# A recurrent attention and two MLPs on one core: fewer operations on the SBUF port that VectorE and GpSimd share, and an order of work that counts that port

## The chip, the cores and the metric

The kernel runs on one NeuronCore of one Trainium2 chip. The metric is the device time of one execution in microseconds (us). Five engines have queues of their own and run them strictly in order: TensorE (PE, with its weight loads shown as PEld), ScalarE (ACT), VectorE (DVE), GpSimd (POOL), and SyncE (SP), which here only starts DMAs.

## The reference

An attention with a matrix state per head (batch 4, 8 heads, 768 steps, head size 40) is followed by two MLPs over the 3072 tokens of width 320:

```python
for t in range(S):
    y[:, :, t] = np.einsum('bhd,bhde->bhe', rt, state)
    Sa = np.einsum('bhde,bhe->bhd', state, at)
    state = state * wt[:, :, None, :] - np.einsum('bhd,bhe->bhde', Sa, bt)
    state = state + np.einsum('bhd,bhe->bhde', vt, kt)
h = np.maximum(x @ w_in, 0.0)
x = h * h @ w_out                      # d_ff 2048
silu = g * (1.0 / (1.0 + np.exp(-g)))  # g = x @ w_gate, val = x @ w_val, d_ff 1536
out = silu * val @ w_out
```

The r, k, v, w, a and b of the attention are float32. The MLP weights reach the kernel as float64, in an array of 64-bit words, and are converted on the chip.

## The kernel before, in words

**Attention.** Time is cut into chunks of 32 steps. One *slot* handles one chunk for half of the batch and all heads. There are 48 slots, and slot i needs the state that slot i-2 left. Ahead of each slot, `e_stage` (L701) loads the decays and a, k, b into a tile called wakb and prepares them: a scan over the decays gives the running products DT (L711), two products give AB ("am", L715), a second, reversed scan over the same decays (L717), a reciprocal of the last running product (L720), a product with it ("rd", L721), and two products that give KB ("km", L724). `inverse` (L755 on) inverts triangular blocks with 30 small VectorE operations (L770, L773) for every window of up to four slots. `slot` then runs the chain on TensorE and VectorE: UQ (L885), TV (L897), ut (L914), the new state ("decay", L916), and the output yb (L954).

**MLP 1** works in 96 *pairs* (12 blocks of 256 tokens by 8 pairs of 128 hidden columns). The operand of every product is split in a rounded high part and a low part, and three products replace one. A pair (`pair1`, L1018) is: 16 matmuls F into one of two PSUM banks (L417), relu from PSUM to the SBUF tile room (L1030), square in SBUF (L1031), the high part gh (a rounding copy, L393), the low part gl = value - gh on GpSimd (`split_pair`, L1013, recorded at L1015), and 12 matmuls O (L422). The PSUM bank is free for the next but one pair as soon as the relu has read it.

**MLP 2** works in 72 pairs of the same kind (`pair2`, L1271 on), with a sigmoid and two VectorE products (L1286, L1288, L1289) in place of relu and square. It runs after the attention's SBUF has been given back. Its weights, converted earlier to float32 in DRAM, are loaded in 48 tiles (`w2_tile`, L1209, low part at L1221).

**Weight conversion.** `conv` (L1070) takes one weight tile of float64 words: 36 tiles for MLP 1 and 36 for MLP 2. `conv_ops` (L366) makes float32 out of the words with eight operations: two on ScalarE (L375, L376), a maximum on VectorE or GpSimd (L377), a shift, a merge and a mask on VectorE (L379, L382, L384), a product and a sum on either engine (L386, L387). ScalarE and GpSimd then make high and low parts ("wh", "wl" at L1099 to L1109).

**The order of the work.** The order in each engine's queue is not written by hand. A planner (`Plan`, L68 on) runs a list schedule when the program is built: each `op` has a cost per engine that may run it, a due time, and the data that it reads and writes. The planner's clock decides which engine gets an operation that several may run, and where in each queue it stands. Its cost formulas are linear in the elements per partition; a scan counts 0.344 us. It treats VectorE and GpSimd as two engines with nothing in common. Nothing of this clock is left at run time, only the order.

Of the kernel before, what the change touches and what calls it, by code (L numbers as in the profile page):

```python
# [57 lines left out]
class Op:  # L58
    __slots__ = ("cost", "fn", "due", "seq", "need", "succ", "ready", "take", "give", "cols", "done", "eng", "tag", "mate", "claim", "dma", "mode", "act")
# [8 lines left out]
class Plan:  # L68
# [14 lines left out]
    def __init__(self):  # L83
# [13 lines left out]
        self.filler = None  # L97

    def op(self, cost, fn, r=(), w=(), due=0.0, dma=0.0, take=None, give=None, cols=0, tag="", mode=None, act=0):
# [224 lines left out]
def tile_kernel(ctx: ExitStack, tc: tile.TileContext, a: dict, out: bass.AP, nb: int, seq: int):  # L324
# [269 lines left out]
    room = mp.tile([128, 5 * BT + 2 * BT + 2 * DM], F32, name="room")  # L594
    gr = [room[:, 2 * n * BT:2 * (n + 1) * BT].rearrange("p (h t) -> p h t", h=2) for n in range(NGR)]
# [2 lines left out]
    os_ = [room[:, 7 * BT + n * DM:7 * BT + (n + 1) * DM] for n in range(2)]
# [2 lines left out]
    xr = room[:, 4 * BT:7 * BT].rearrange("p (k t) -> p k t", k=3)
# [892 lines left out]
```

## Time and profile before

| what | value |
|---|---|
| three runs | 1331.74, 1333.31, 1334.23 us (median 1333.31) |
| span of the profiled execution, first to last instruction | 1322.9 us |
| median less that span | 10.4 us |
| granted TensorE clock, mean | 0.952 of full speed |
| instructions | 47171 |

The profiled execution has no time of its own beside its span. The median lies 10.4 us above the span, and that difference stands for what lies around the span. "Idle before, releaser" in a row is the time that the engine sat idle in front of these instructions, and what ended most of it. A releaser is the one that came last by the profile.

### The profile page before, as it was taken

The numbers are of one execution on the slowest core, as the hardware profiler recorded it, in microseconds if no ns is written. First come the engines' busy times: TensorE is split into PE (matmuls) and PEld (weight loads), VectorE is DVE, ScalarE is ACT, GpSimd is POOL, SyncE is SP. The second block draws the span as 40 slices with busy tenths as digits, with TensorE's granted clock in tenths as the row PEclk, the third lists the DMA queues.
The fourth block names the chain that finished last, engine by engine and source line by source line (L and its number), as shares of the span: only waits on it lengthen the run. The fifth ranks groups of instructions, "written<-read, shape, count | busy, mean of one in ns | idle before, by whom it ended". The sixth has DMA issues, their size and how long they took to land. (4 is left out here: it accounts for less than half of the span.)

```text
span 1322.9 us, 47171 instructions
## 1 busy us (share of the span) xinstructions
PE 1148.5 (87%) x20302; PEld 1068.8 (81%) x20302; DVE 668.4 (51%) x1557; ACT 551.4 (42%) x1342; POOL 502.8 (38%) x515
## 2 busy tenths in 40 slices
PE   3257678888979898999899999978999999999997
PEld 2146677777867787888788888977999999999996
DVE  7897797937485948463535331144322222222221
ACT  3344555544445555444444444555322222222221
POOL 6556655635443545343444312222222222222221
PEclk9999787989978989899999989988999999999999
DMA  6354545653636454534343322234000001001000
GB/s 178 99 143 106 154 108 138 154 135 87 177 103 173 113 153 126 137 91 120 74 119 78 80 60 64 75 100 133 20 23 23 23 23 23 23 23 23 11 11 13
DMA packets 173121, 116.29 MB, mean 88 GB/s; under 512 B 105704, under 2 KB 148968, under 8 KB 172904
## 3 DMA queue, kind: packets, MB, share of 16 engines
q1 hardware_dynamic: 172904, 113.19, 33.1%
q8 instruction: 161, 2.64, 0.9%
q14 instruction: 56, 0.46, 0.1%
HBM read 89.14 MB, written 23.99 MB: 86 GB/s over the span
## 5 line engine op out<-in xcount | busy, mean ns | idle before, releaser
L1015 POOL TENSOR_TENSOR gl<-room,gh 128x512 fp32r<-128x512 f32 x168 | 220.1, 1310 | 527.8 <-ACT gh L393 492.1
L1288 DVE TENSOR_TENSOR room<-ps,room 128x512 f32<-128x512 f32 x72 | 49.8, 692 | 222.3 <-ACT room L1286 222.2
L393 ACT CAST gh<-room 128x512 fp32r<-128x512 f32 x168 | 104.6, 623 | 105.7 <-DVE room L1289 103.4
L422 PE MATMUL ps<-o1h,gh 128*128 128x320 f32 x384 | 139.1, 362 | 1.8 <-ACT gh L393 1.8
L422 PE MATMUL ps<-o1h,gl 128*128 128x320 f32 x384 | 126.1, 328 | 2.4 <-POOL gl L1015 2.3
L417 PE MATMUL ps<-xh,w1h 128*128 128x256 f32 x384 | 121.8, 317 | 6.2 <-ACT room L1030 6.2
L422 PE MATMUL ps<-o1l,gh 128*128 128x320 f32 x384 | 125.4, 327 | 0.0
L715 POOL TENSOR_TENSOR AB<-wakb,DT 40x256 f32<-40x256 f32 x88 | 82.5, 937 | 112.3 <-DVE DT L711 33.7
L417 PE MATMUL ps<-xl,w1h 128*128 128x256 f32 x384 | 111.7, 291 | 0.8 <-DVE xl L983 0.7
L417 PE MATMUL ps<-xh,w1l 128*128 128x256 f32 x384 | 111.5, 290 | 0.2 <-issue 0.2
L1286 ACT ACTIVATE room<-ps 128x512 f32<-128x512 f32 x72 | 43.1, 598 | 143.0 <-PE ps L417 110.0
L422 PE MATMUL ps<-o2h,gl 128*128 128x320 f32 x288 | 89.4, 310 | 0.9 <-POOL gl L1015 0.9
L422 PE MATMUL ps<-o2h,gh 128*128 128x320 f32 x288 | 89.2, 310 | 0.3 <-ACT gh L393 0.3
L422 PE MATMUL ps<-o2l,gh 128*128 128x320 f32 x288 | 89.0, 309 | 0.0
L417 PEld LDWEIGHTS ps<-xh,w1h 128*128 128x128 f32 x384 | 75.9, 198 | 10.9 <-ACT room L1030 6.6
L422 PEld LDWEIGHTS ps<-o1h,gh 128*128 128x128 f32 x384 | 78.0, 203 | 7.5 <-ACT gh L393 2.0
L724 POOL TENSOR_TENSOR KB<-wakb 104x256 f32<-104x256 f32 x89 | 65.6, 757 | 47.4 <-PE ps L837 45.8
L422 PEld LDWEIGHTS ps<-o1h,gl 128*128 128x128 f32 x384 | 78.5, 204 | 4.1 <-POOL gl L1015 3.8
L417 PE MATMUL ps<-xh,wgh 128*128 128x256 f32 x288 | 81.0, 281 | 0.0
L417 PE MATMUL ps<-xh,wvh 128*128 128x256 f32 x288 | 80.0, 278 | 0.0
L417 PE MATMUL ps<-xl,wgh 128*128 128x256 f32 x288 | 79.9, 277 | 0.0
L417 PE MATMUL ps<-xh,wgl 128*128 128x256 f32 x288 | 79.9, 277 | 0.0
(177 smaller groups left out, 3381.6 us busy)
## 6 DMA issues: line engine op xcount, KB each, us to landing
wakb<-in_wakb_dram SPq DMA_DIRECT2D x46, 422.5 KB
RB<-in_vr_e_dram SPq DMA_DIRECT2D x48, 208.0 KB
RH<-in_r_e_dram SPq DMA_DIRECT2D x96, 80.0 KB
cx<-in_moe_w_out_dram SPq DMA_DIRECT2D x24, 320.0 KB
room<-xt_d SPq DMA_DIRECT2D x36, 128.0 KB
TV<-in_v_t_dram SPq DMA_DIRECT2D x192, 20.0 KB
cx<-in_moe_w_in_dram SPq DMA_DIRECT2D x15, 256.0 KB
xt_d<-yb SPq DMA_DIRECT2D x24, 160.0 KB
```

The lines of the kernel that those rows point to most:

```text
L393: nc.scalar.copy(dst, src) if e == ACT else eng[e].tensor_copy(dst, src)
L417: nc.tensor.matmul(ps, w[:, c], x, start=(i == 0), stop=(i == len(seq_) - 1))
L422: nc.tensor.matmul(acc[t][:, :DM], g[:, half, ts], w[:, f, :], start=(f == 0 and i == 0), stop=(f == nf - 1 and i == 2),)
L715: att(two, lambda e, q=q, b=b: eng[e].tensor_mul(ab[b:b + D, q], ah[b:b + D], d[b:b + D, :, 0:C]), ((ka0, ka1)[q], ("DT", nd)), (("AB", g ...
L724: att(two, lambda e, k=k, n=n: eng[e].tensor_mul(kb[:, :, k * C:(k + 1) * C], akb[:, n], rd), (kw, kk), (("KB", nk),), due=due + 0.3, tag= ...
L1015: op({POOL: t_pool(512)}, lambda e: eng[e].tensor_sub(gl[n], gr[n], gh[n].bitcast(F32)), (("gr", n), ("gh", n)), (("gl", n),), due=due, ta ...
L1286: op({ACT: 0.478}, lambda e: nc.scalar.activation(gr[n], two["pg"][b], AF.Sigmoid), (("pg", b),), (("gr", n),), due=due, tag="sig")
L1288: op({DVE: 0.602}, lambda e: nc.vector.tensor_mul(gr[n], two["pg"][b], gr[n]), (("pg", b),), (("gr", n),), due=due, tag="ug")
```

## The change

In words, part by part:

1. **The planner counts the port.** Operations get a flag `port`. Every GpSimd operation and every flagged VectorE operation (two inputs from SBUF, or a conversion step) now exclude each other on the planner's clock. A scan's cost goes from 0.344 to 0.617 us for 264 elements. Several operations that only GpSimd could run (am, km, wl, gl of MLP 2) may now go to either engine.
2. **Conversion of float64 words.** The mask and the product are gone, and the sum becomes one whole-number addition on GpSimd: the low word, scaled by 2^-29 and rounded to a whole number by ScalarE, is added to the merged high word.
3. **MLP 1 stays in PSUM.** relu and square run in place in the PSUM bank, gh is rounded from it, and gl is now a VectorE operation that reads PSUM and gh. The bank is free when gl has read it.
4. **e_stage.** The reciprocal goes into a second constant tile c2, at the places where the reversed scan restarts, so that the scan starts from 1/D. The product rd is gone.
5. **Buffers.** MLP 1 needs no SBUF tile for a pair's values; MLP 2 takes two from the attention's space. Conversion has four input buffers throughout, in place of five for the first 24 tiles and three afterwards.

```diff
+def t_scan(n):
+    return 0.068 + 0.00208 * n
...
     def at(self, o, e):
         t = o.ready[e]
+        if self.shares(o, e):
+            t = max(t, self.port)
...
+    def shares(o, e):
+        return e == POOL or (e == DVE and o.port)
...
         self.free[e] = t + d
+        if self.shares(o, e):
+            self.port = t + d
...
-            ({ACT: t_act(n)}, lambda e: nc.scalar.activation(lo_f, lo_u, AF.Copy, scale=2.0 ** -52), "x", "l"),
+            ({ACT: t_act(n)}, lambda e: nc.scalar.activation(lo_i, lo_u, AF.Copy, scale=2.0 ** -29), "x", "l"),
...
-            ({DVE: t_dve2(n)}, lambda e: nc.vector.tensor_scalar(
-                out=hi_i, in0=t, scalar1=-0x800000, scalar2=None, op0=ALU.bitwise_and), "t", "h"),
-            (two, lambda e: eng[e].tensor_mul(lo_f, lo_f, hi_f), "lh", "l"),
-            (two, lambda e: eng[e].tensor_add(t.bitcast(F32), t.bitcast(F32), lo_f), "tl", "t"),
+            ({POOL: t_pool(n)}, lambda e: nc.gpsimd.tensor_tensor(out=t, in0=t, in1=lo_i, op=ALU.add), "tl", "t"),
...
-    NCX, NCT = 3, 3
+    NCX, NCT = 4, 4
...
-        two = {POOL: t_pool(8 * C), DVE: t_dve(8 * C)} if g < EARLY else {POOL: t_pool(8 * C)}
+        two = {POOL: t_pool(8 * C), DVE: t_dve(8 * C)}
...
-        att({DVE: 0.12}, lambda e: nc.vector.reciprocal(RD, d[:, :, C]), (("DT", nd),), ("RD",), due=due, tag="rec")
-        att(two, lambda e: eng[e].tensor_mul(rd, rd, RD[:, :, None].to_broadcast([EPAD, 8, C])),
-            ("RD",), (kw,), due=due, tag="rd")
+        att({DVE: 0.12}, lambda e: nc.vector.reciprocal(c2_[:, C + 1:nw + 1:C + 1], d[:, :, C]), (("DT", nd),), ("c2",),
+            due=due, tag="rec")
+        att({DVE: t_scan(nw)}, lambda e: nc.vector.tensor_tensor_scan(
+            w[:, nw:0:-1], w[:, nw:0:-1], c2_[:, nw:0:-1], initial=0.0, op0=ALU.mult, op1=ALU.add),
+            ("c2",), (kw,), due=due, tag="scan", port=True)
...
     def split_pair(n, due):
-        op({POOL: t_pool(512)}, lambda e: eng[e].tensor_sub(gl[n], gr[n], gh[n].bitcast(F32)),
-           (("gr", n), ("gh", n)), (("gl", n),), due=due, tag="gl")
+        op({POOL: t_pool(512), DVE: t_dve(512)}, lambda e: eng[e].tensor_sub(gl[n], two["gr"][n], gh[n].bitcast(F32)),
+           (("gr", n), ("gh", n)), (("gl", n),), due=due, tag="gl", port=True)
...
-        op({ACT: 0.478}, lambda e: nc.scalar.activation(gr[n], P1[b], AF.Relu), (("p", b),), (("gr", n),), due=due, tag="relu")
-        op({ACT: 0.52}, lambda e: nc.scalar.activation(gr[n], gr[n], AF.Square), (), (("gr", n),), due=due, tag="sqr")
-        split_pair(n, due)
+        for f in (AF.Relu, AF.Square):
+            op({ACT: 0.478}, lambda e, f=f: nc.scalar.activation(P1[b], P1[b], f), (), (("p", b),), due=due, tag="relu")
+        op({ACT: 0.478}, lambda e: copy(e, gh[n], P1[b]), (("p", b),), (("gh", n),), due=due, tag="gh")
+        op({DVE: t_dve(512)}, lambda e: split_lo(gl[n], P1[b], gh[n]), (("p", b), ("gh", n)), (("gl", n),), due=due, tag="gl")
```

The order moves everywhere, since the planner's clock moved. Three places show it. In all of them wakb, DT, AB and KB are tiles of e_stage, and cx and ct tiles of the conversion. Line numbers of the changed kernel are its own.

GpSimd in the middle of the attention. Before:

```order
L715 TENSOR_TENSOR AB_149<-wakb_169,DT_139 40x256 x2
L386 TENSOR_TENSOR cx_117<-cx_117 128x320
L387 TENSOR_TENSOR ct_120<-ct_120,cx_117 128x320
L721 TENSOR_TENSOR wakb_169<-wakb_169,rd 104x8x32
L1015 TENSOR_TENSOR gl_109<-room,gh_107 128x512
L724 TENSOR_TENSOR KB_137<-wakb_169 104x8x32 x2
L715 TENSOR_TENSOR AB_150<-wakb_170,DT_140 40x256 x2
L721 TENSOR_TENSOR wakb_170<-wakb_170,rd 104x8x32
L724 TENSOR_TENSOR KB_138<-wakb_170 104x8x32 x2
```

The changed kernel, in about the same slots (L397 is the whole-number addition, L390 the maximum, L730 one km):

```order
L397 TENSOR_TENSOR ct_119<-ct_119,cx_116 128x320
L397 TENSOR_TENSOR ct_120<-ct_120,cx_117 128x320
L397 TENSOR_TENSOR ct_121<-ct_121,cx_118 128x320
L397 TENSOR_TENSOR ct_122<-ct_122,room 128x320
L397 TENSOR_TENSOR ct_119<-ct_119,cx_116 128x320
L390 TENSOR_SCALAR ct_121<-ct_121 128x320
L397 TENSOR_TENSOR ct_120<-ct_120,cx_117 128x320
L390 TENSOR_SCALAR ct_122<-ct_122 128x320
L730 TENSOR_TENSOR KB_136<-wakb_170 104x8x32
L397 TENSOR_TENSOR ct_121<-ct_121,cx_118 128x320
```

The e_stage products and the low parts gl have left this queue; additions of the conversion fill it.

VectorE in the same part of the program, around one e_stage. Before (L379 to L384, L387 and L377 are conversion):

```order
L954 TENSOR_TENSOR yb_178<-ps,DT_143 104x2x4x32
L711 SCALAR_TENSOR_TENSOR DT_143<-wakb_169,c_179 104x264
L717 SCALAR_TENSOR_TENSOR wakb_169<-wakb_169,c_179 104x264
L720 RECIPROCAL rd<-DT_143 104x8
L387 TENSOR_TENSOR ct_120<-ct_120,cx_117 128x320
L377 TENSOR_SCALAR ct_121<-ct_121 128x320
L379 TENSOR_SCALAR ct_121<-ct_121 128x320
L382 SCALAR_TENSOR_TENSOR ct_121<-cx_118,ct_121 128x320
L384 TENSOR_SCALAR cx_118<-ct_121 128x320
```

The changed kernel (L378 is gl of a pair, L722 am, L730 km):

```order
L750 TENSOR_TENSOR L_129<-ps,mask 128x256
L378 TENSOR_TENSOR gl_109<-ps,gh_107 128x512
L819 TENSOR_TENSOR P_133<-P_133,ps 128x4x16
L903 TENSOR_SCALAR TV_162<-ps 32x8x40
L920 TENSOR_TENSOR ut<-ps,ST_156 104x320
L922 TENSOR_TENSOR ST_156<-ut,DT_145 104x2x4x40
L960 TENSOR_TENSOR yb_178<-ps,DT_144 104x2x4x32
L718 SCALAR_TENSOR_TENSOR DT_144<-wakb_170,c_179 104x264
L722 TENSOR_TENSOR AB_148<-wakb_170,DT_144 40x256 x2
L724 RECIPROCAL c_180<-DT_144 104x8
L726 SCALAR_TENSOR_TENSOR wakb_170<-wakb_170,c_180 104x264
L730 TENSOR_TENSOR KB_138<-wakb_170 104x8x32 x2
```

am, km and gl now stand in this queue between UQ, TV, ut and the state, and mask, product and sum have gone.

ScalarE near the end of the attention, where the last pairs of MLP 1 run and the weights of MLP 2 arrive (ws are the tiles that are loaded). Before:

```order
L1030 ACTIVATE room<-ps 128x512
L1031 ACTIVATE room<-room 128x512
L393 CAST gh_108<-room 128x512
L1030 ACTIVATE room<-ps 128x512
L1031 ACTIVATE room<-room 128x512
L393 CAST gh_107<-room 128x512
L1030 ACTIVATE room<-ps 128x512
L1031 ACTIVATE room<-room 128x512
L393 CAST xh_112<-room 128x768
L393 CAST gh_108<-room 128x512
L1030 ACTIVATE room<-ps 128x512
L1031 ACTIVATE room<-room 128x512
```

The changed kernel (L1037 is relu or square, L403 a copy or rounding):

```order
L1037 ACTIVATE ps<-ps 128x512 x2
L403 CAST gh_107<-ps 128x512
L1037 ACTIVATE ps<-ps 128x512 x2
L403 CAST gh_108<-ps 128x512
L403 CAST xh_112<-room 128x768
L1037 ACTIVATE ps<-ps 128x512 x2
L403 CAST wgh_13472<-ws_13462 128x256
L403 CAST wgh_13473<-ws_13463 128x256
L403 CAST wghl<-ws_13464 128x256
L403 CAST gh_107<-ps 128x512
```

relu and square have PSUM on both sides now, and gh reads the bank; between a pair's square and its gh stand three weight tiles.

## Rows read from the trace of the kernel before

**Rows 1.** The page, part 1: busy time, share of the span and instructions of each engine.
```profile
PE 1148.5 (87%) x20302; PEld 1068.8 (81%) x20302; DVE 668.4 (51%) x1557; ACT 551.4 (42%) x1342; POOL 502.8 (38%) x515
```

**Rows 2.** Busy time by stretch: from:to us, length, each engine, clock, DMA share, GB/s.
```profile
0.00:186.00 186.00, 101.92 (x2620) 86.61 (x2620) 154.84 (x414) 79.21 (x232) 110.74 (x134) 0.94 0.51 132
186.00:544.00 358.00, 307.97 (x7328) 273.99 (x7314) 247.72 (x596) 181.68 (x483) 175.40 (x186) 0.91 0.51 134
544.00:829.00 285.00, 266.51 (x6477) 240.84 (x6476) 121.29 (x325) 132.29 (x330) 99.62 (x104) 0.96 0.36 90
829.00:909.00 80.00, 69.87 (x644) 66.78 (x643) 23.89 (x43) 42.42 (x90) 20.97 (x16) 0.91 0.32 91
909.00:1323.00 414.00, 402.26 (x3256) 400.59 (x3254) 120.65 (x183) 115.80 (x212) 96.04 (x75) 0.99 0.11 26
```

**Rows 3.** Timeline of VectorE, UQ of slots 8 and 28: start, duration, line, operands.
```profile
185.73 0.31 DVE L885 TENSOR_TENSOR UQ<-ps,UV 128x160 f32<-128x160 f32 x1
...
543.55 0.33 DVE L885 TENSOR_TENSOR UQ<-ps,UV 128x160 f32<-128x160 f32 x1 [3.21 <-PE ps L881]
```

**Rows 4.** VectorE group, 0 to 186 us: busy, mean ns, idle before and releaser.
```profile
L386 DVE TENSOR_TENSOR cx<-cx 128x256 f32<-128x256 f32 (+1 forms) x20 | 11.3, 564 | 0.1
```

**Rows 5.** Single lines, whole run: count, shortest/median/longest ns, first and last start.
```profile
L386 DVE TENSOR_TENSOR cx<-cx x51: 411/483/2210, 30.4 to 561.6; 128x320 f32<-128x320 f32 x36, 128x256 f32<-128x256 f32 x15
...
L384 DVE TENSOR_SCALAR cx<-ct x63: 279/321/1408, 30.0 to 561.2; 128x320 int32<-128x320 int32 x48, 128x256 int32<-128x256 int32 x15
...
L715 DVE TENSOR_TENSOR AB<-wakb,DT x4: 409/420/422, 7.7 to 10.9; 40x256 f32<-40x256 f32 x4
...
L1221 DVE TENSOR_TENSOR wvl<-ws,wvh x12: 418/426/1372, 862.9 to 910.6; 128x256 fp32r<-128x256 f32 x12
...
L1288 DVE TENSOR_TENSOR room<-ps,room x72: 677/692/693, 920.2 to 1309.3; 128x512 f32<-128x512 f32 x72
...
L773 DVE TENSOR_TENSOR qt<-qt,tmp x195: 164/210/1328, 34.9 to 767.0; 128x15 f32<-128x15 f32 x22, 128x28 f32<-128x28 f32 x22, 128x39 f32<-128x39 f32 x22, 128x48 f32<-128x48 f32 x22
...
L387 POOL TENSOR_TENSOR ct<-ct,cx x13: 746/877/1167, 34.8 to 509.2; 128x320 f32<-128x320 f32 x10, 128x256 f32<-128x256 f32 x3
```

**Rows 6.** Timeline, a VectorE and a GpSimd operation together; below, L916 over the run.
```profile
410.62 1.49 DVE L916 TENSOR_TENSOR ST<-ut,DT 104x320 f32<-104x320 f32 x1
...
410.47 1.29 POOL L1015 TENSOR_TENSOR gl<-room,gh 128x512 fp32r<-128x512 f32 x1 [3.22 <-DMA TV<-in_v_t_dram]
...
L916 DVE TENSOR_TENSOR ST<-ut,DT x44: 475/493/1593, 66.7 to 794.5; 104x320 f32<-104x320 f32 x44
```

**Rows 7.** VectorE groups, 186 to 544 us.
```profile
L773 DVE TENSOR_TENSOR qt<-qt,tmp 128x15 f32<-128x15 f32 (+7 forms) x75 | 28.9, 386 | 1.3
...
L916 DVE TENSOR_TENSOR ST<-ut,DT 104x320 f32<-104x320 f32 x19 | 13.9, 732 | 0.3
```

**Rows 8.** GpSimd group of gl, 186 to 544 us, then 544 to 829 us.
```profile
L1015 POOL TENSOR_TENSOR gl<-room,gh 128x512 fp32r<-128x512 f32 x40 | 53.6, 1341 | 56.4 <-ACT gh L393 50.7 <-DMA TV<-in_v_t_dram 4.6 <-PE ps L911 0.6
...
L1015 POOL TENSOR_TENSOR gl<-room,gh 128x512 fp32r<-128x512 f32 x37 | 48.6, 1313 | 107.6 <-ACT gh L393 91.5 <-issue 9.7 <-DVE tmp L770 6.3
```

**Rows 9.** TensorE waits (us, times, longest), 0 to 186 us, then 186 to 544 us.
```profile
PE ps L741 <- POOL KB L724: 25.4, 4, 19.4
...
PE ps L890 <- DVE UQ L885: 12.8, 7, 3.0
...
PE ps L890 <- DVE tmp L770: 8.1, 2, 4.7
```

**Rows 10.** ScalarE groups over the run: gh and relu.
```profile
L393 ACT CAST gh<-room 128x512 fp32r<-128x512 f32 x168 | 104.6, 623 | 105.7 <-DVE room L1289 103.4 <-PE ps L422 1.1
...
L1030 ACT ACTIVATE room<-ps 128x512 f32<-128x512 f32 x96 | 56.7, 591 | 50.0 <-PE ps L417 48.2 <-POOL gl L1015 1.5
```

**Rows 11.** Chain of waits, 836 to 846 us: start, us, 16 F and 12 O.
```profile
841.54 2.11 PE ps L417 x16
843.65 1.76 PE ps L422 x12
```

More of the change, by code (lines that the diff above doesn't have):

```diff
@@ L58 @@
 class Op:
-    __slots__ = ("cost", "fn", "due", "seq", "need", "succ", "ready", "take", "give", "cols", "done", "eng", "tag", "mate", "claim", "dma", "mode", "act")
+    __slots__ = ("cost", "fn", "due", "seq", "need", "succ", "ready", "take", "give", "cols", "done", "eng", "tag", "mate", "claim", "dma", "mode", "act", "port")
 class Free:
@@ L97, in __init__, with op @@
         self.filler = None
-    def op(self, cost, fn, r=(), w=(), due=0.0, dma=0.0, take=None, give=None, cols=0, tag="", mode=None, act=0):
+        self.port = 0.0
+    def op(self, cost, fn, r=(), w=(), due=0.0, dma=0.0, take=None, give=None, cols=0, tag="", mode=None, act=0, port=False):
         o = Op()
@@ L102, in op @@
         self.n += 1
-        o.dma, o.claim, o.mode, o.act = dma, None, mode, act or cols
+        o.dma, o.claim, o.mode, o.act, o.port = dma, None, mode, act or cols, port
         o.succ, o.done, o.eng, o.mate = [], None, None, None
@@ L167, in at @@
         return t
+    @staticmethod
+    def shares(o, e):
+        return e == POOL or (e == DVE and o.port)
     def pe_time(self, o, t):
@@ L593, in tile_kernel @@
     NGR = 2
[L594 to L595 removed]
+    nwa = NWA + 24 * C
+    room = mp.tile([128, 2 * nwa], F32, name="room")
     gh = ring(mp, NGR, [128, 2, BT], F32R, "gh")
     gl = ring(mp, NGR, [128, 2, BT], F32R, "gl")
[L598 removed]
+    os_ = [room[:, 3 * BT + n * DM:3 * BT + (n + 1) * DM] for n in range(2)]
     xhs = ring(mp, 2, [128, 3, BT], F32R, "xh")
     xls = ring(mp, 2, [128, 3, BT], F32R, "xl")
[L601 removed]
+    xr = room[:, 0:3 * BT].rearrange("p (k t) -> p k t", k=3)
     PS = psa.tile([128, 8, 512], F32, name="ps")
@@ L916, in slot @@
             att({DVE: 0.4, POOL: 0.83} if i >= SPREAD else {DVE: 0.4}, lambda e: eng[e].tensor_mul(stv, ut, decay),
-                ("tt", ("DT", nd)), (Ts,), due=due, tag="decay")
+                ("tt", ("DT", nd)), (Ts,), due=due, tag="decay", port=True)
         def z_mm(tag):
@@ L1088, in conv @@
                     ks += kxs if c == "x" else [names[c]]
-                op(cost, fn, ks, [names[c] for c in wr], due=due, tag="conv")
+                op(cost, fn, ks, [names[c] for c in wr], due=due, tag="conv", port=True)
         if store:
@@ L1196, in open_in @@
         two["x"] = ring(sp2, 4, [128, 384], F32, "x2")
+        two["gr"] = ring(sp2, NGR, [128, 2, BT], F32, "gr")
         two["w"] = Weights2(wp2, None)
@@ L1221, in low @@
             eng[e].tensor_sub(d, s, h.bitcast(F32))
-        op({POOL: t_pool(n), DVE: t_dve(n)}, low, ks + [kh, "W2"], (wkey(key),), due=due, tag="wl")
+        op({POOL: t_pool(n), DVE: t_dve(n)}, low, ks + [kh, "W2"], (wkey(key),), due=due, tag="wl", port=True)
     for g in range(NP2):
@@ L1285, in pair2 @@
                    due=due, cols=2048, tag="F2")
-        op({ACT: 0.478}, lambda e: nc.scalar.activation(gr[n], two["pg"][b], AF.Sigmoid), (("pg", b),), (("gr", n),),
-           due=due, tag="sig")
-        op({DVE: 0.602}, lambda e: nc.vector.tensor_mul(gr[n], two["pg"][b], gr[n]), (("pg", b),), (("gr", n),), due=due, tag="ug")
-        op({DVE: 0.602}, lambda e: nc.vector.tensor_mul(gr[n], two["pv"][b], gr[n]), (("pv", b),), (("gr", n),), due=due, tag="uv")
+        kw = dict(due=due)
+        op({ACT: 0.478}, lambda e: nc.scalar.activation(two["gr"][n], two["pg"][b], AF.Sigmoid), (("pg", b),), (("gr", n),),
+           tag="sig", **kw)
+        for q in ("pg", "pv"):
+            op({DVE: 0.602}, lambda e, q=q: nc.vector.tensor_mul(two["gr"][n], two[q][b], two["gr"][n]), ((q, b),), (("gr", n),),
+               tag="u" + q, **kw)
         split_pair(n, due)
```

63 lines of the change are left out of this document (26 added, 37 removed).

## The prediction

> **What bounds the kernel now.** I read the page first, then the busy time by stretch, the TensorE and VectorE rows of each stretch, and last single operations on the timeline. On the whole span TensorE is busy 87%, VectorE 51%, GpSimd 38% [rows 1], which names no bound, since the stages differ. The five stretches [rows 2] are cut where slot 8 and slot 28 begin [rows 3], near slot 47, and where MLP 2 takes over.
>
> - Start, 0 to 186 us, slots 0 to 7: VectorE is busy 154.8 of 186 us, TensorE 101.9. MLP 1 cannot run yet, because its weights are still being converted. VectorE sets the pace here.
> - Middle, 186 to 544 us, slots 8 to 27: TensorE is busy 308.0 of 358 us at a granted clock of 0.91. A slot takes 358 / 20 = 17.9 us. Conversion of MLP 2's weights runs beside it.
> - Late, 544 to 829 us, 19 slots: TensorE is busy 266.5 of 285 us, clock 0.96; 285 / 19 = 15.0 us a slot.
> - Passage, 829 to 909 us: the last pairs of MLP 1 while MLP 2's weights arrive. TensorE is busy 69.9 of 80.
> - MLP 2, 909 us to the end: TensorE is busy 402.3 of 414 us. Nothing that another engine does matters here.
>
> So there is time to win in the start and the middle, and little after 544 us.
>
> **The port, as the rows show it.** The new state (L916) takes 0.49 us at the median and up to 1.59. In the collision shown it starts 0.15 us after a GpSimd gl and ends 0.35 us after that gl has ended, 1.49 us in all, while the gl takes its usual 1.29 [rows 6]. An operation with a PSUM input does not show this: L1288 lies between 0.677 and 0.693 in all 72 cases [rows 5]. In the middle stretch L773 averages 0.386 against a median of 0.210, and L916 0.732 [rows 5, 6, 7]: 75 x 0.176 + 19 x 0.239 = 17.7 us of blocked VectorE time in these two groups alone. So a GpSimd operation is paid for twice, on GpSimd and by whichever VectorE operation comes then.
>
> **Part by part.** The counts are of the changed order and the one before.
>
> *Start.* Up to the UQ of slot 8 VectorE loses 31 masks, 27 products, 26 sums and 3 rd: 31 x 0.321 + 53 x 0.483 (a sum counted as a product) + 3 x 0.42 = 10.0 + 25.6 + 1.3 = 36.9 us. It gains 21 am, 19 km, 24 wl, 7 maxima and 3 gl: 40 x 0.420 + 24 x 0.426 + 7 x 0.32 (as the mask) + 3 x 0.692 = 31.3 us [rows 5]. Net -5.6 us. The blocked time is the larger part: a product averages 0.564 here against 0.483 [rows 4, 5], a factor 1.17, so of 154.8 us some 22 are blocked time, as an estimate. GpSimd, busy 110.7 us here, loses all that VectorE gains, so I take two thirds of the 22 away, 15 us. Sum -20 us. The scan that starts from 1/D has 264 elements and two SBUF inputs as before, one of them wider; I count 0, at most 13 x 0.1 us in either direction. TensorE also waited 25.4 us for KB from GpSimd's queue [rows 9], part of the same 20. Bounds: 0, if the conversion's loads set the pace instead, and -45, this 20 and the 25.4 in full.
>
> *Middle.* VectorE loses 39 masks, 29 products, 29 sums, 11 maxima, 5 shifts and 5 merges, 12.5 + 14.0 + 14.0 + about 7.5 = 48 us, and gains 79 am and km, 39 gl from PSUM and 7 wl, 33.2 + 27.0 + 3.0 = 63 us. With its blocked time it was busy 247.7 us. If two thirds of the blocked time goes, and that is 50 us as an estimate (the two groups' 17.7 on 42.8 us busy, the others less hit), it ends near 230, or 64% of the stretch: not a bound. What counts is what TensorE gets: it idles 50 us here, 20.9 of that for UQ and for operations of the inverse in front of UQ [rows 9]. At the late pace the 20 slots take 20 x 15.0 = 300 us, 58 less. I take a little over half, -32 us, since conversion still runs beside it and since gl and am now sit in the queue of UQ. Bounds -58 and -10.
>
> The SBUF — State Buffer page of the Trainium skill, section Who interferes with whom, says that an operation on the shared port holds it for its whole length and the other engine waits. By that rule alone I would add GpSimd's 175.4 us to VectorE's two-input work: the pair of engines would be near full before and near half full after, and the middle would run at the late pace, -58 us, a sum of -81. The trace agrees on who waits in the collision [rows 6], but TensorE's own idle time says how much of it reaches the end, so the sum keeps -32.
>
> *Late.* gl (37) and am, km (51) go to VectorE, 25.6 + 21.4 = 47 us, on top of 121.3 of 285. Covered by 285 - 168 us of idle VectorE; without the cover each gl would hold TV or UQ by 0.69 us. L916 loses its collisions. -5 us, bounds -12 and +3.
>
> *Passage.* The PSUM bank of a pair is now free after relu, square, gh and gl, 2 x 0.591 + 0.623 + 0.692 = 2.5 us of work (the square counted as the relu, both from PSUM) and some 0.6 of hand-over (an estimate from the gaps), in place of 0.591 [rows 5, 10]. Attention hides that in the slots. In the passage only F and O run: 16 F take about 1.9 us and 12 O 1.76 [rows 11], so O of a pair comes 3.1 - 1.9 = 1.2 us after the F of the next: 7 times for 14 pairs, taken two at a time, 8 us. Against it TensorE idled 10 us here anyway and the weight tiles' low parts lose collisions with gl. +3 us, bounds -5 and +10.
>
> *MLP 2.* gl moves from 1.29 us on GpSimd to about 0.62 on VectorE (512 elements between the 0.42 of 256 and the 0.69 from PSUM), under a busy TensorE: only the last pair shows, -1 us.
>
> *Whole-number addition.* 72 on GpSimd at 0.877, the float sum's median there; between that and its longest, 1.167 [rows 5], or a little below. Even 1.167 adds 0.3 x 72 = 21 us on an engine that is mostly idle. I count 0. More than 3 us each would matter, as then 36 of them outlast the start.
>
> Sum: -20 - 32 - 5 + 3 - 1 = **-55 us**. Span 1322.9 - 55 = 1268; plus 10.4 around it, the distance of the median from the span, **1278 us**.
>
> **Rivals.**
>
> 1. *VectorE waits for ScalarE in GpSimd's place (slower).* gl used to stand in GpSimd's queue, which stood idle in front of it until gh came: 50.7 us in the middle and 91.5 us late [rows 8]. Now gl stands in the queue of UQ, TV and the state. If VectorE stands as long and TensorE inherits all of it, that is +142 us: 1420. Half of it is +71, 1349. It decides from 55 / 142 = 39% on. For it: 76 gl in these stretches, in front of the attention's chain. Against it: in the changed order gl is placed after the operations that are ready earlier, and VectorE has a third of its time free. [...]
> 2. *Everything runs at the late pace.* Start -45, middle -58, late -8, the rest +2: -109, or 1224. For it: blocked time is spread over all of the start and middle. Against it: conversion still loads and still occupies ScalarE as it did. The rule of the SBUF page above leads to the middle part of this rival.
> 3. *TensorE takes it all back (no change).* The order still reaches only as far as ScalarE and the clock allow, and the waits move to relu and gh. Start -8, the rest +8: 1333. Against it: TensorE idles 84 us in the start and 50 in the middle.
> 4. *The change does not do what it says.* The planner's clock may be wrong in another place, and operations stand in an order that blocks; that gives the times of rivals 1 or 3.
>
> **How the numbers follow.** Forecast (a gain of 15 to 90 us): 0.70. Rival 1: 0.14. Rival 2: 0.11. Rivals 3 and 4 at no change: 0.05. Of the forecast's bounds, the sum of all the good ends is -121 and of all the bad ends +3; not all come together. The range for 8 in 10 goes from 1230, which takes in most of rival 2's way, to 1326. 0.2% is 2.7 us, about what a measurement of this kernel can tell from no change. Faster 0.81, same 0.04, slower 0.15.
>
> **What would show it.** In the changed profile GpSimd should fall from 503 to under 200 us, L773 and L916 of the changed kernel should average near their medians of 0.21 and 0.49, and slot 8 should begin near 166 us, slot 28 near 492, the last F of MLP 1 near 855. MLP 2 should keep its 414 us. VectorE busy above 85% in the middle, or TensorE waiting longer than 40 us there for UQ or TV behind a gl, would mean rival 1. A slot of 17.9 us in the middle as before would mean that the port was not the cause.

## The result and the profile after

The changed kernel takes 1300.28 us (median of 4 runs, 1297.79 to 1302.61) against 1333.18 us for the kernel before on the same chip: a ratio of 0.9764, interval 0.9738 to 0.9789, or 32.9 us less. The forecast was 1278 us with a range of 1230 to 1326. The sign and the range were right, the size was not: 55 us were forecast.

A profile is one execution, and executions of one kernel on one chip lie up to 9 us apart for the changed kernel (a_self below) and up to 18 us for the kernel before (25 executions). The profiled execution of the changed kernel took 1300.57 us for a span of 1298.3, so 2.3 us lie around the span. The span before was 1322.9, so span against span the change is worth 24.6 us; the steps below are held against those 24.6. A stage's length in one profile is good to some us: slot 8 began at 173.5 us here and at 176.4 in a second profile of the same kernel.

Page of the changed kernel, part 1, which answers to [rows 1]:

```profile
PE 1148.6 (88%) x20308; PEld 1068.7 (82%) x20308; DVE 692.2 (53%) x1736; ACT 541.8 (42%) x1342; POOL 128.4 (10%) x145
```

GpSimd falls from 502.8 to 128.4 us. VectorE is busier than before, 692.2 against 668.4, and the kernel is still faster, so its total is not what counts. TensorE's busy time is the same, 1148.6 against 1148.5 us: all 24.6 us are idle time of TensorE, 149.7 us in place of 174.4. By stretch, cut as in [rows 2] (from:to, length, PE, PEld, DVE, ACT, POOL, clock, DMA share, GB/s):

```profile
0.00:173.50 173.50, 102.51 (x2651) 86.70 (x2652) 128.39 (x396) 77.98 (x233) 50.67 (x67) 0.97 0.53 136
173.50:507.50 334.00, 301.64 (x7284) 269.83 (x7284) 217.02 (x607) 173.90 (x470) 64.23 (x65) 0.91 0.53 138
507.50:799.00 291.50, 268.33 (x6473) 241.88 (x6472) 152.15 (x423) 131.35 (x342) 11.77 (x11) 0.95 0.39 98
799.00:884.00 85.00, 70.46 (x628) 66.27 (x629) 28.73 (x61) 39.63 (x88) 0.00 (x0) 0.90 0.31 94
884.00:1298.30 414.30, 405.64 (x3285) 403.99 (x3283) 165.91 (x253) 118.94 (x213) 1.75 (x2) 0.99 0.09 24
```

The first two cuts are the UQ of slots 8 and 28 on VectorE's timeline (start, duration), as in [rows 3]:

```profile
173.53 0.32 DVE L891 TENSOR_TENSOR UQ<-ps,UV 128x160 f32<-128x160 f32 x1
...
507.55 0.31 DVE L891 TENSOR_TENSOR UQ<-ps,UV 128x160 f32<-128x160 f32 x1
```

| stretch | before, us | after, us | difference | forecast |
|---|---|---|---|---|
| start | 186 | 173.5 | -12.5 | -20 |
| middle | 358 | 334 | -24 | -32 |
| late | 285 | 291.5 | +6.5 | -5 |
| passage | 80 | 85 | +5 | +3 |
| MLP 2 | 413.9 | 414.3 | +0.4 | -1 |

The last cut is not at one event: cut at the first matmul with MLP 2's weights (913.8 and 891.1 us), the passage grows by 7.1 us and MLP 2 shrinks by 1.9.

VectorE loses 26.4 us of busy time in the start and 30.7 in the middle; it gains 30.9 late and 45.3 in MLP 2. The collisions are nearly gone. VectorE's groups in the middle, 173.5 to 507.5 us (busy, mean ns, idle before and releaser), against [rows 7]:

```profile
L378 DVE TENSOR_TENSOR gl<-ps,gh 128x512 fp32r<-128x512 f32 x39 | 26.7, 686 | 10.5 <-ACT gh L403 10.2
L722 DVE TENSOR_TENSOR AB<-wakb,DT 40x256 f32<-40x256 f32 x39 | 20.5, 526 | 0.6
...
L779 DVE TENSOR_TENSOR qt<-qt,tmp 128x28 f32<-128x28 f32 (+7 forms) x78 | 16.5, 212 | 0.7
```

The inverse's subtraction averages 0.212 us instead of 0.386; 0.210 is its median [rows 5, 7]. *Held-up time* is, in what follows, each VectorE operation's time above the tenth percentile of its line and shape, summed over the operations that stand alone, not directly beside one of their own kind. It falls from 122 us (37 in the start, 62 in the middle, 19 late, 5 after) to 33 (13.5, 13.7, 4.3, 1). With the others too it is 127 and 41: am, which now runs on VectorE, averages 0.526 us in the middle against the 0.420 that the prediction counted. So some 90 us of held-up time went, and the kernel gained 25 to 33 us. How much of the gain comes from it is what the experiments are for.

What TensorE waited for (us, times, longest), in the start, the middle, the late stage and the passage:

```profile
PE ps L747 <- DVE KB L730: 32.5, 7, 12.9
...
PE ps L803 <- DMA p1t<-p_d: 7.0, 5, 2.6
...
PE ps L917 <- DVE TV L903: 7.4, 4, 3.8
...
PE ps L432 <- ACT gh L403: 13.7, 4, 5.1
```

In the middle the 20.9 us in front of UQ [rows 9] are gone, and the longest entry is now a transfer. TensorE idles 32.4 us there, against 50. In the start it waits for KB from VectorE. That is not more than before: to the 25.4 us for KB from GpSimd [rows 9] the start before adds a second entry, for KB from VectorE, and the two make 38.4:

```profile
PE ps L741 <- DVE KB L724: 13.0, 2, 11.9
```

In the passage it waits for gh.

### The profile page after: what moved, and what is told of

Read it like the earlier page. It is cut to its first block, busy times and chain, and to the rows that moved or that the text cites. A ratio compares the mean times of both kernels' runs of the same rounds, so it can differ in the third digit from the quotient of the medians.

```text
span 1298.3 us, 46776 instructions
## 1 busy us (share of the span) xinstructions
PE 1148.6 (88%) x20308; PEld 1068.7 (82%) x20308; DVE 692.2 (53%) x1736; ACT 541.8 (42%) x1342; POOL 128.4 (10%) x145
## 4 chain that ended last, share of the span: by engine, by line
PE 56%; DMA 21%; DVE 7%; SPq 6%; issue 5%; ACT 4%; POOL 1%; DVEq 0%; ACTq 0%; POOLq 0%
PE ps L427 27%; PE ps L432 18%; SPq L679 5%; DMA room<-xt_d 3%; DMA wakb<-in_wakb_dram 3%; DMA ws<-f_moe_w_val 2%; DMA TV<-in_v_t_dram 2%; DMA xi<-xi_d 2%; PE ps L955 1%; DMA cx<-in_moe_w_in_dram 1%; DMA p1t<-p_d 1%; DMA xt_d<-yb 1%; ACT ps L1037 1%; PE ps L936 1%; PE ps L809 1%
## 5 line engine op out<-in xcount | busy, mean ns | idle before, releaser
L1295 DVE TENSOR_TENSOR gr<-ps,gr 128x512 f32<-128x512 f32 x144 | 99.6, 692 | 192.9 <-ACT gr L1292 185.4
L432 PE MATMUL ps<-o1h,gh 128*128 128x320 f32 x384 | 141.7, 369 | 13.8 <-ACT gh L403 13.7
L1037 ACT ACTIVATE ps<-ps 128x512 f32<-128x512 f32 x192 | 112.6, 587 | 66.1 <-PE ps L427 64.5
L1292 ACT ACTIVATE gr<-ps 128x512 f32<-128x512 f32 x72 | 43.2, 600 | 149.4 <-PE ps L427 149.3
L378 DVE TENSOR_TENSOR gl<-ps,gh 128x512 fp32r<-128x512 f32 x96 | 66.0, 688 | 73.9 <-ACT gh L403 73.1
L432 PEld LDWEIGHTS ps<-o1h,gh 128*128 128x128 f32 x384 | 78.8, 205 | 21.3 <-ACT gh L403 15.3
L403 ACT CAST gh<-gr 128x512 fp32r<-128x512 f32 x72 | 44.7, 621 | 93.6 <-DVE gr L1295 92.5
L432 PEld LDWEIGHTS ps<-o1l,gh 128*128 128x128 f32 x384 | 79.9, 208 | 0.0
L427 PE MATMUL ps<-xl,wvh 128*128 128x256 f32 x288 | 79.5, 276 | 0.0
```

The costliest lines, as they stand in the source:

```text
L378: nc.vector.tensor_sub(dst, full, hi.bitcast(F32))
L403: nc.scalar.copy(dst, src) if e == ACT else eng[e].tensor_copy(dst, src)
L427: nc.tensor.matmul(ps, w[:, c], x, start=(i == 0), stop=(i == len(seq_) - 1))
L432: nc.tensor.matmul(acc[t][:, :DM], g[:, half, ts], w[:, f, :], start=(f == 0 and i == 0), stop=(f == nf - 1 and i == 2),)
L1037: op({ACT: 0.478}, lambda e, f=f: nc.scalar.activation(P1[b], P1[b], f), (), (("p", b),), due=due, tag="relu")
L1292: op({ACT: 0.478}, lambda e: nc.scalar.activation(two["gr"][n], two["pg"][b], AF.Sigmoid), (("pg", b),), (("gr", n),), tag="sig", **kw)
```

## The experiments

Twelve kernels ran on two chips, each beside the kernel before. "Held up" is the first sum above (122 and 33 us), from each one's profiled execution; GpSimd is its busy time there.

| kernel | ratio to before, 95% interval | GpSimd, us | VectorE held up, us |
|---|---|---|---|
| b_model | 0.9983, 0.9956 to 1.0011 | 469 | 116 |
| b_psum | 0.9989, 0.9960 to 1.0017 | 397 | 84 |
| b_conv | 1.0059, 1.0031 to 1.0087 | 517 | 122 |
| b_e | 0.9865, 0.9834 to 0.9896 | 377 | 107 |
| b_memset | 0.9859, 0.9813 to 0.9905 | 456 | 84 |
| a_noport | 0.9862, 0.9822 to 0.9903 | 172 | 54 |
| a_conv | 0.9950, 0.9919 to 0.9981 | 121 | 28 |
| a_epool | 0.9860, 0.9795 to 0.9925 | 252 | 63 |
| a_self | 0.9783, 0.9745 to 0.9821 | 129 | 33 |
| a_late | 0.9757, 0.9718 to 0.9795 | 141 | 39 |
| a_nogh | 0.9739, 0.9699 to 0.9780 | 129 | 33 |
| a_add | 0.9734, 0.9695 to 0.9773 | 85 | 17 |

Held-up time alone does not order these kernels: b_psum and b_memset both have 84 us, and one gains nothing, the other 1.4%.

**One part alone, on the kernel before.** b_model lets the planner count the port and the longer scan, with every operation as it was:

```
+        if self.shares(o, e):
+            t = max(t, self.port)
...
-        att({DVE: 0.344}, lambda e: nc.vector.tensor_tensor_scan(
+        att({DVE: t_scan(nw)}, lambda e: nc.vector.tensor_tensor_scan(
```

> The kernel before with only the planner's new view: the port flags and the scan cost of 0.617 us, every operation as it was (GpSimd-only operations stay GpSimd-only). If the order by itself made the gain, about 1300 us as the whole change. If the gain is blocked VectorE time that goes with the operations on GpSimd, most of those operations are still here: between 1320 and 1333 us.

1332.11 us, no difference that can be told. With GpSimd still at 469 us the planner can move work but not remove it, and held-up time stays at 116.

b_psum squares MLP 1's pairs in PSUM and takes their low parts on VectorE from there:

```
-        op({ACT: 0.478}, lambda e: nc.scalar.activation(gr[n], P1[b], AF.Relu), (("p", b),), (("gr", n),), due=due, tag="relu")
...
+        for f in (AF.Relu, AF.Square):
+            op({ACT: 0.478}, lambda e, f=f: nc.scalar.activation(P1[b], P1[b], f), (), (("p", b),), due=due, tag="relu")
...
+        op({DVE: t_dve(512)}, lambda e: split_lo(gl[n], P1[b], gh[n]), (("p", b), ("gh", n)), (("gl", n),), due=due, tag="gl")
```

> The kernel before with only the pairs of MLP 1 kept in PSUM and their low part gl on VectorE; the planner is as before. Theory of blocked time: 96 GpSimd operations of 1.3 us and their collisions go, 96 VectorE operations of 0.69 us come: 1315 to 1325 us. Rival that VectorE waits for gh in front of UQ and TV: no gain or slower, 1333 to 1350 us.

1334.87 us, no difference. VectorE's groups in its middle, 187 to 543 us:

```profile
L364 DVE TENSOR_TENSOR gl<-ps,gh 128x512 fp32r<-128x512 f32 x40 | 27.4, 684 | 12.0 <-ACT gh L393 11.8
...
L773 DVE TENSOR_TENSOR qt<-qt,tmp 128x15 f32<-128x15 f32 (+7 forms) x75 | 20.4, 272 | 1.0
```

L773 is less held up than in [rows 7], 0.272 us against 0.386. But VectorE gives what it gains back: 38 us less held up over the run, 66 us of its own for 96 gl of 0.69, and 11.8 us of waiting for gh in the middle alone. (VectorE has 72 operations more, not 96: the planner moved 24 others to GpSimd.)

b_conv has only the whole-number addition:

```
-            (two, lambda e: eng[e].tensor_mul(lo_f, lo_f, hi_f), "lh", "l"),
-            (two, lambda e: eng[e].tensor_add(t.bitcast(F32), t.bitcast(F32), lo_f), "tl", "t"),
+            ({POOL: t_pool(n)}, lambda e: nc.gpsimd.tensor_tensor(out=t, in0=t, in1=lo_i, op=ALU.add), "tl", "t"),
```

> The kernel before with only the whole-number addition in the conversion. VectorE loses about 35 us in the start and 40 us in the middle, where the start is VectorE's: theory of VectorE as the bound of the start: 1315 to 1325 us. If the start is paced by something else: within 3 us of 1333.

1343.16 us, slower by 0.6%, although VectorE's total falls to 617.5 us, as the page's part 1 shows:

```profile
PE 1163.6 (87%) x20300; PEld 1083.1 (81%) x20300; DVE 617.5 (46%) x1382; ACT 553.2 (41%) x1342; POOL 516.6 (38%) x546
```

The addition has GpSimd as its only engine, where gl, am and km stand too. Held-up time stays at 122 us. So less VectorE work, by itself, buys nothing, and not in the start either. There VectorE is busy 141.7 us, 13 less than before, and GpSimd 118, 7 more; slot 8 begins when it did [rows 3]:

```profile
186.40 0.31 DVE L881 TENSOR_TENSOR UQ<-ps,UV 128x160 f32<-128x160 f32 x1
```

Why it lost time is not settled: its middle is 13.6 us longer, of which 9 are TensorE's own busy time at a granted clock of 0.89 against 0.91; TensorE's waits for UQ there are 15.3 us against 12.8 [rows 9].

b_e seeds the backward scan with 1/D, drops rd, and lets VectorE take am and km:

```
-        two = {POOL: t_pool(8 * C), DVE: t_dve(8 * C)} if g < EARLY else {POOL: t_pool(8 * C)}
+        two = {POOL: t_pool(8 * C), DVE: t_dve(8 * C)}
...
-            w[:, nw:0:-1], w[:, nw:0:-1], c1[:, nw:0:-1], initial=0.0, op0=ALU.mult, op1=ALU.add),
+            w[:, nw:0:-1], w[:, nw:0:-1], c2_[:, nw:0:-1], initial=0.0, op0=ALU.mult, op1=ALU.add),
...
-        att(two, lambda e: eng[e].tensor_mul(rd, rd, RD[:, :, None].to_broadcast([EPAD, 8, C])),
```

> The kernel before with only e_stage changed: the scan starts from 1/D, rd is gone, am and km may go to either engine by the planner's old costs. The old planner will put some of them on VectorE. Theory of blocked time: 48 rd and part of 190 GpSimd products go: 1318 to 1328 us. If moving work to VectorE in its full start costs as much as it frees: within 5 us of 1333 or slower.

1318.68 us, 1.35% less: the only part that gains alone. Held-up time falls by 15 us only, so it is not that alone: 44 rd are gone from the attention's chain, and the short chain to AB and KB no longer stands behind GpSimd's gl. Which of the two did it was not tried apart.

**The port by itself.** b_memset keeps the order of the kernel before, and each gl on GpSimd becomes two fills that only write:

```
-        op({POOL: t_pool(512)}, lambda e: eng[e].tensor_sub(gl[n], gr[n], gh[n].bitcast(F32)),
+        op({POOL: t_pool(512)}, lambda e: [nc.gpsimd.memset(gl[n].bitcast(F32), 0.0) for _ in range(2)],
```

> The kernel before in its own order; each gl of both MLPs on GpSimd is replaced by two memsets of the same tile, which write SBUF and read nothing. The low part of the product operands is left out of the computation. GpSimd is occupied for about the same time (two memsets of 512 elements against one 1.29 us operation), but no longer reads SBUF beside VectorE. Theory of blocked time: L916 and the inverse operations lose their collisions with gl in the middle and late stages; 8 to 20 us faster than before, 1313 to 1325 us. If the collisions lie off the path that sets the end: within 3 us of 1333.

1308.70 us, 1.4% less, with the same work on VectorE, in the same order. VectorE's groups in its middle, 184 to 532 us:

```profile
L773 DVE TENSOR_TENSOR qt<-qt,tmp 128x28 f32<-128x28 f32 (+7 forms) x76 | 21.3, 281 | 1.3
L916 DVE TENSOR_TENSOR ST<-ut,DT 104x320 f32<-104x320 f32 x19 | 10.3, 540 | 0.3
```

0.386 becomes 0.281 and 0.732 becomes 0.540 [rows 7], though GpSimd is still busy 456 us. The timeline shows both cases in 2 us: the first operation of the inverse starts during a GpSimd product and ends just after it, the next two run at their usual length while GpSimd fills.

```profile
360.08 0.77 POOL L386 TENSOR_TENSOR cx<-cx 128x320 f32<-128x320 f32 x1 [1.37 <-ACT room L1030]
360.79 1.10 POOL L1015 MEMSET gl<- 128x512 f32 x2
...
360.42 0.49 DVE L770 TENSOR_TENSOR tmp<-qt,xi 128x39 f32<-128x39 f32 x1
360.94 0.20 DVE L773 TENSOR_TENSOR qt<-qt,tmp 128x39 f32<-128x39 f32 x1
361.17 0.21 DVE L770 TENSOR_TENSOR tmp<-qt,xi 128x48 f32<-128x48 f32 x1
```

Of the 195 L773, the 32 that start during a fill take at most 0.004 us more than the median of their shape; the 31 that start during a GpSimd TENSOR_TENSOR take 0.376 more on average. So it is not GpSimd's being busy that holds VectorE up, but operations that read.

How much of the 1.4% that is worth is less clear, since a fill also does not wait for gh and leaves the low parts at zero. Of the 21.1 us between the two profiles, 10.3 lie in the middle and 2.7 in the late stage, but 6.5 lie behind slot 47, where little was held up before (5 us). In the middle 4.8 of the 10.3 us are shorter busy time of TensorE, at a granted clock of 0.93 against 0.91.

**One part undone, on the changed kernel.** a_noport blinds the planner to the port again and gives the scan its old cost:

```
-    return 0.068 + 0.00208 * n
+    return 0.344
...
-        return e == POOL or (e == DVE and o.port)
+        return False
```

> The changed kernel with all its operations, but a planner that does not count the port and takes a scan for 0.344 us as before. If operations make the gain: within 5 us of 1300. If the planner's view is needed for it: 1310 us or more.

1309.62 us, ratio 0.9862: the planner's rule with the scan's cost, worth nothing alone, is worth about 1% here. GpSimd takes 172 us instead of 128, held-up time is 54 instead of 33. The stages of its profile differ both ways. The start loses its gain, as slot 8 begins at 185.46 us; the late stage is 11 us shorter than the changed kernel's:

```profile
185.46 0.31 DVE L891 TENSOR_TENSOR UQ<-ps,UV 128x160 f32<-128x160 f32 x1
...
524.20:804.40 280.20, 265.37 (x6481) 237.79 (x6481) 143.07 (x391) 126.13 (x327) 9.98 (x13) 0.98 0.36 87
```

a_conv goes back to the conversion of eight steps:

```
-            ({POOL: t_pool(n)}, lambda e: nc.gpsimd.tensor_tensor(out=t, in0=t, in1=lo_i, op=ALU.add), "tl", "t"),
...
+            (both, lambda e: eng[e].tensor_mul(lo_f, lo_f, hi_f), "lh", "l"),
+            (both, lambda e: eng[e].tensor_add(t.bitcast(F32), t.bitcast(F32), lo_f), "tl", "t"),
```

> The changed kernel with the conversion of before (mask, product and sum in place of the whole-number addition). Theory of blocked time and of VectorE as the bound of the start: 8 to 20 us slower than the changed kernel, 1308 to 1320 us. If the conversion is hidden: within 4 us of 1300.

1322.85 us, ratio 0.9950. With VectorE at 722 us most of the gain is lost although it is held up for only 28: that fits VectorE's own work as the limit once little holds it up, but no run shows it apart. (The profiled execution was 1309.65 us, the lowest of ten, so its stage lengths are not used.)

a_epool gives am and km of the later groups back to GpSimd:

```
-        two = {POOL: t_pool(8 * C), DVE: t_dve(8 * C)}
+        two = {POOL: t_pool(8 * C), DVE: t_dve(8 * C)} if g < EARLY else {POOL: t_pool(8 * C)}
```

> The changed kernel with am and km on GpSimd alone from the fourth e_stage on, as before; the scan still starts from 1/D. 180 products of 0.42 us leave VectorE and 180 of 0.69 to 0.82 us come back to GpSimd with their collisions. Theory of blocked time: 5 to 15 us slower than the changed kernel, 1305 to 1315. If VectorE's queue is what holds the middle and late stages (the rival), faster than 1300.

1306.96 us, ratio 0.9860 with a wide interval. Held-up time doubles to 63 us; a loss of 0.8 to 1% against the changed kernel is likely, no more than that.

**What is left in the changed kernel.** Four kernels ran on one chip: the changed kernel again, with no edit, and three beside it.

> The changed kernel itself, as the measure for the three beside it, since single executions of one kernel lie up to 8 us apart. Every theory: ratio to the kernel before 0.974 to 0.979. If the late stage's 291 us (before: 285) was one execution's accident, it shows here as 280 to 286; if it belongs to the order, as 289 to 298.

1307.04 us, ratio 0.9783. Its middle and late stretches have the lengths of the first profile:

```profile
176.00:509.00 333.00, 304.18 (x7300) 272.35 (x7288) 217.12 (x608) 174.27 (x469) 64.37 (x65) 0.89 0.53 138
509.00:800.00 291.00, 263.88 (x6497) 237.31 (x6485) 153.10 (x423) 131.82 (x344) 11.39 (x11) 0.98 0.40 98
```

So the late 291 us belong to the kernel. They came out the same at a granted clock of 0.98 as at 0.95: TensorE's idle time made up the difference, 27 us against 23.

a_late counts the port for early operations alone:

```
-        return e == POOL or (e == DVE and o.port)
+        return o.due < 28 and (e == POOL or (e == DVE and o.port))
```

> The changed kernel with the port counted by the planner only for operations due before slot 28, and not after. Theory A (the late stage is longer because a planner that counts the port in it holds operations back that hardly meet there): late stage 280 to 286 us in place of 291, start and middle as in the changed kernel, ratio to the changed kernel 0.991 to 0.996. Theory B (stage lengths of one profile are only good to some 8 us, and the order does not matter there): ratio to the changed kernel 0.998 to 1.002, with a late stage on either side.

1306.33 us, 0.998 of a_self (interval 0.996 to 1.001), late stage 288 us. The ratio is theory B's: counting the port late costs nothing that can be told. But start and middle did not stay as they were, as theory A wanted them: slot 28 begins at 520.2 us in its profile, against 507.5 and 509.4 in the two of the changed kernel. And the run shows something it was not made for. VectorE hardly waits for gh in its late stage (us, times, longest, 520.2 to 808.3 us), and TensorE's idle time there stays as it was, 22.4 us against 23.2:

```profile
DVE gl L378 <- ACT gh L403: 2.2, 5, 1.2
...
520.20:808.30 288.10, 265.65 (x6450) 239.65 (x6451) 145.66 (x399) 130.98 (x332) 18.25 (x20) 0.96 0.38 94
```

a_nogh was to take VectorE's wait for gh away, with the order kept:

```
-        op({DVE: t_dve(512)}, lambda e: split_lo(gl[n], P1[b], gh[n]), (("p", b), ("gh", n)), (("gl", n),), due=due, tag="gl")
+        op({DVE: t_dve(512)}, lambda e: split_lo(gl[n], P1[b], gl[n]), (("p", b), ("gh", n)), (("gl", n),), due=due, tag="gl")
```

> The changed kernel in the same order, with VectorE's low part of MLP 1's pairs worked out from the pair and its own old value and so not waiting for ScalarE's high part (it leaves the true low part out). It takes away VectorE's 66 us of waiting for the high part (10 in the middle, 41 in the late stage, 15 in the passage). Theory A (my first rival, in small: VectorE's queue stands behind that wait and TensorE pays): 8 to 25 us faster than the changed kernel, most of it in the late stage and the passage, ratio to it 0.981 to 0.994. Theory B (TensorE is the bound at the clock it is granted, VectorE has the slack): within 4 us, ratio 0.997 to 1.003.

It missed its aim. The wait stayed, as VectorE's waits show (us, times, longest):

```profile
DVE gl L378 <- ACT gh L403: 71.3, 48, 5.6
```

a_self has 75.8 there. ScalarE's copy and VectorE's subtraction both read the pair's bank, and the program orders one behind the other even when VectorE does not need the result: in all 96 pairs the subtraction starts after the copy's end. So this run does not price the wait. The run has another use: with the wait in place it is nearly the changed kernel again, and it reads 1303.00 us, 0.996 of a_self (0.993 to 0.999). Differences of 0.4% are not to be read here.

a_add makes the whole-number addition two fills that only write:

```
-            ({POOL: t_pool(n)}, lambda e: nc.gpsimd.tensor_tensor(out=t, in0=t, in1=lo_i, op=ALU.add), "tl", "t"),
+            ({POOL: t_pool(n)}, lambda e: (nc.gpsimd.memset(lo_i, 0), nc.gpsimd.memset(t[:, 0:1], 0)), "tl", "lt"),
```

> The changed kernel in the same order, with GpSimd's whole-number add of the conversion (72 of them, some 0.98 us each) replaced by two fills that only write and don't hold VectorE up (it leaves the low words of the weights out). Of VectorE's held-up time of 33 us that is left in the changed kernel it takes most of what lies in the first two stages (13.5 and 13.7 us). Theory A (blocked time still reaches the end, at about the rate of 25 us for 90 as between the two kernels): 5 to 10 us faster, ratio to the changed kernel 0.992 to 0.996. Theory B (what is left is covered): within 3 us, ratio 0.998 to 1.002.

1300.74 us, 0.995 of a_self (0.992 to 0.998), but 0.998 of a_nogh. Held-up time halves, 33 to 17 us; a gain of 0 to 6 us cannot be told more closely. Whatever the port still costs is small.

No kernel that computes everything beats the changed one by more than these runs can tell.

## Why the prediction was right in its sign and too large

- **The port: right, its share of the gain open.** The forecast stood on VectorE's operations being held up. b_memset shows directly that GpSimd's reads do that, in one order and with the same VectorE work. The amount was there too: 22 and 50 us estimated in the start and middle, 37 and 62 by the sum over the trace, of which 63% and 78% went (two thirds forecast). GpSimd under 200 us, the averages of L773 and L916 near their medians, VectorE well under 85% in the middle (217 of 334): all as forecast. Slots 8 and 28 came later than forecast, 173.5 and 507.5 us for 166 and 492. What held-up time is worth in us is not shown by any run by itself. The prediction's estimate from the SBUF — State Buffer page of the Trainium skill, section Who interferes with whom, was -58 us for the middle; -24 was measured, so the rule names the mechanism but not how much of it reaches the end.
- **Start, -20 forecast, -12.5 measured.** VectorE freed itself of 26.4 us, about the 21 forecast, but the start did not follow. The step that failed is "VectorE sets the pace here", taken from its busy time: b_conv took 13 us of busy time from VectorE in the start, and slot 8 began at 186.4 us as before. The 25.4 us wait for KB from GpSimd [rows 9], counted as part of the gain, was 38.4 us with KB from VectorE; 32.5 of them are left, all for VectorE. The wait moved to the engine that km moved to. The start's gain goes with the planner's view: a_noport, with the same operations, has none of it. The planner's view changes both the order and which engine takes an operation, and which of the two makes the gain is open.
- **Middle, -32 forecast, -24 measured.** The waits that the sum named went. The step that failed is the floor. I took the late pace of 15.0 us a slot, 58 us less, as what could be reached, and a little over half of it. But TensorE alone was busy 308.0 us for the 20 slots [rows 2], 15.4 us each, at a granted clock of 0.91; it still is, 301.6 us at 0.91. So no more than its idle 50 us were to be had from waits. Of these 17.7 were got. The other 6.3 came from shorter busy time, and that is work moved elsewhere: 37.5 pairs' F and 38.0 pairs' O lie in this stretch, against 39.5 of each before, at 2.1 and 1.8 us [rows 11]. Half of 50 instead of 58 would have been -25 to -28.
- **Late, -5 forecast, +6.5 measured.** Here the sign was wrong. "Covered by idle VectorE" left out that gl waits. VectorE stands for gh in the late stage and in the middle (us, times, longest):

```profile
DVE gl L378 <- ACT gh L403: 40.9, 27, 3.9
...
DVE gl L378 <- ACT gh L403: 10.2, 12, 1.9
```

  That is rival 1 in small: 51.1 us in place of GpSimd's 142 [rows 8], 36%. It put the point of decision at 39% of the 142 us and TensorE inheriting all of that, but TensorE inherited little: its late idle time went from 18.5 to 23.2 us, with 7.4 us waiting for TV. Nor do the runs bear out that this wait lengthens the stage. Where it is nearly gone (a_late, 2.2 us) TensorE idles 22.4 us; where it is as long (a_noport, 38.4 us) TensorE idles 14.8 us, and the stage takes 280 us at a granted clock of 0.98, against 291 and 27 us of idle time at 0.98 in a_self. Since a_noport has the changed kernel's operations, the late 291 us go with the order and the choice of engines that the planner makes when it counts the port. Counting it up to slot 28 alone (a_late) does not win the 11 us back. Which part of the order it is stays open.
- **Passage, +3 forecast, +5 measured**, within its bounds, but not as described. The sum had seven gaps of 1.2 us, since the pair's bank is free only after relu, square, gh and gl. (Its 1.9 us for 16 F is 2.11 in [rows 11], which makes the gaps 1.0.) TensorE waits 13.7 us in four places, up to 5.1, for gh itself, which stands in ScalarE's queue behind MLP 2's weight tiles and their transfers. In the first of them, after relu and square (start, duration):

```profile
826.20 1.19 ACT L1037 ACTIVATE ps<-ps 128x512 f32<-128x512 f32 x2
827.31 0.70 ACT L403 CAST wgh<-ws 128x256 fp32r<-128x256 f32 x2
828.98 0.41 ACT L403 CAST wghl<-ws 128x256 fp32r<-128x256 f32 x1 [0.97 <-DMA ws<-f_moe_w_gate]
829.29 0.58 ACT L403 CAST gh<-ps 128x512 fp32r<-128x512 f32 x1
```

  The term came out near for another reason: that is luck.
- **MLP 2, -1 forecast, +0.4 measured** (-1.9 with the other cut). gl takes 0.692 us from SBUF, not the estimated 0.62, under a busy TensorE.
- **Whole-number addition, counted at 0.** Its median was 0.978 us, not 0.877, and the longest 1.862, above the 1.167 taken as the upper end. The price itself was right: six of 128x320 that no VectorE operation overlaps take 0.86 to 0.88 us, and the rest is collisions. (The prediction's limit of 3 us each is too low: 36 of them are 108 us, and the start lasts 173.) GpSimd was idle enough to carry that, and a_add bounds what is left at 6 us. But counting it alone hid that the parts are not additive: alone it costs 0.6%, undone it loses most of the gain.
- **10.4 us around the span: wrong.** It is 2.3 here, and some 1.9 in the other executions of the kernel before. The profiled execution of before was some 8 us below its median, which is why the medians differ by 32.9 and the spans by 24.6.

The ratios also show that the parts work together. The four parts alone sum to -1.04% (-0.17, -0.11, +0.59, -1.35); together they give -2.2 to -2.4%. That fits a planner's rule that needs operations which can go to either engine, and a VectorE that can take them only once the conversion's steps are gone. It is not shown: the fifth part of the change, the buffers, was tried by no run of its own.

## What to carry to other kernels

Before a stretch is given a gain from another stretch's pace, divide the bound engine's own busy time by the number of slots: its idle time in that stretch, not the difference of paces, is the most that removing waits can give. When an operation moves to another engine's queue, move its wait with it, and then ask whether the bound engine idles for it: with or without 41 us of it on VectorE, TensorE idled the same here. Before a wait is counted as a gain, add up its entries for all the engines that make the data. Parts that free one shared resource are not additive: test each alone and each undone, since a rule that is worth nothing alone was worth 1% in company.

## What the runs showed of the hardware that was not expected

A collision can be paid by GpSimd too. Single lines of the changed kernel (count, shortest/median/longest ns, first and last start):

```profile
L397 POOL TENSOR_TENSOR ct<-ct,cx x54: 731/978/1817, 45.6 to 560.8; 128x320 int32<-128x320 int32 x39, 128x256 int32<-128x256 int32 x15
...
L397 POOL TENSOR_TENSOR ct<-ct,room x18: 737/932/1862, 50.5 to 595.8; 128x320 int32<-128x320 int32 x13, 128x256 int32<-128x256 int32 x5
...
L922 DVE TENSOR_TENSOR ST<-ut,DT x44: 466/491/1196, 57.3 to 780.8; 104x320 f32<-104x320 f32 x44
...
L1021 DVE TENSOR_TENSOR gl<-gr,gh x72: 680/692/695, 898.4 to 1287.7; 128x512 fp32r<-128x512 f32 x72
...
L1037 ACT ACTIVATE ps<-ps x192: 545/582/607, 132.9 to 886.8; 128x512 f32<-128x512 f32 x192
```

GpSimd's additions, of two sizes, spread from 0.73 to 1.86 us, the longer ones where VectorE operations with two inputs from SBUF run beside them, while gl before averaged 1.31 to 1.34 [rows 8] and let VectorE pay [rows 6]. A fill of GpSimd that only writes hardly holds VectorE up: with 456 us of GpSimd work, L916 averaged 0.540 us in b_memset's middle, against a median of 0.493 before [rows 6]. VectorE takes 0.692 us for 128x512 from SBUF as from PSUM. And ScalarE in place in PSUM averages 0.587 us over the 192 (median 0.582), against 0.591 for relu from PSUM to SBUF [rows 10].
